# Another order of tasks, and other engines for some of them, in a planned attention and channel-mix kernel

## Chip, core and metric

One core of a Trainium2 chip runs the whole kernel. The metric is the device time in microseconds of one execution; lower is better. The engines are named as in the profile: PE (TensorE), DVE (VectorE), ACT (ScalarE), POOL (GpSimd) and SP (SyncE, which here only issues DMAs).

## What is computed

Block-causal attention over 8 batches, 8 heads, 576 positions and head size 64, and then a channel mix over the attention's output, whose channels are the heads side by side (512).

```python
scores = scale * np.matmul(q, k.transpose(0, 1, 3, 2))
mask = block_i >= block_j                       # blocks of 64 positions
attn = softmax(where(mask, scores, -1e9))
x = (attn @ v).transpose(0, 2, 1, 3).reshape(B, S, H * D)

xk = mu_k * x + (1.0 - mu_k) * x_prev           # x_prev: one position earlier
xr = mu_r * x + (1.0 - mu_r) * x_prev
k = np.maximum(xk @ w_k, 0.0)                   # 512 -> 1024
v = k * k @ w_v                                 # 1024 -> 512
r = 1.0 / (1.0 + np.exp(-(xr @ w_r)))
out = r * v                                     # float32
```

## The kernel before

The kernel is a list of 914 tasks. A task is a few instructions on one engine: a load, a cast, a transpose, a block of matmuls, an exponential. The Python code creates the tasks with what they depend on; two tables then say what is issued. `ORDER` is a list of task numbers: the order in which tasks are issued, and so the order on each engine, which works through its own instructions in that order. A number after a plus sign is a count of fill matmuls (`unread`, L258) on the identity that are put in front of that PE task and whose result nobody reads. `PLACE` has one letter for each task that can run on more than one engine (P for POOL, D for DVE, A for ACT). Buffers come from rings (`RINGS`); a task takes the longest-free slot of a ring at the moment it is issued, so the order decides the slots as well.

The tasks of one batch, by the names used below:

- **Loads** (L266, on SP) of q, k, v and of the weights into one ring of six buffers, `ld`. A buffer is free when its cast is done, and SP issues in order, so a load that waits for a buffer holds all later loads and the stores of the output (L702).
- **Casts** (L245 on ACT, L249 on DVE or POOL, L246 and L250 with a scale) of q and k to bfloat16 (`t_nl`), of v (`t_vo`) and the weights (`WK`, `WR`, `WV`) to float16.
- **Turns** (L332, DVE): 32x32 transposes that bring q and k to head size by position (`t_qkt`).
- **Scores** (L398, PE) into PSUM ring `s` (three buffers), and **exponentials** (L410, ACT) into `t_e`. Batch 0 is done in two parts (positions 0 to 255, and 256 to 575), the others in one, with six units of scores for a batch.
- **Sums** (L460, PE) of the exponentials, a transpose (L486), a reciprocal (L508), small copies (L245 or L249 on `t_rc`) and a second transpose (L533), all on DVE but for some copies; **value groups** A and B (L472, PE); **normalisation** (L543, L547, DVE) into `t_xt`, which gives the PSUM buffers back.
- **Mix**: a difference of neighbouring positions (L570, POOL or DVE), and eight products (L586, DVE) into `XK` and `XR`. They need the mu rows: loaded by L278 (SP, `MUR`), transposed by one small matmul (L285, PE), and shifted by L290 (DVE).
- **Channel mix**: `pk` (L639, PE), **relu** (L612 ACT, L614 DVE), **square** (L621 ACT, L623 DVE or POOL) into `K`; `pr` (L660, PE) and **tanh** (L669, ACT); `pv` (L688, PE), the output product (L696, DVE) and the store. `pk`, `pr` and `pv` share two PSUM buffers, the ring `mm`; relus write a ring `kr` of four.

[...]

Of the kernel before, what the change touches and what calls it, by code (L numbers as in the profile page):

```python
# [19 lines left out]


ORDER = """
# [50 lines left out]
"""  # L73


PLACE = (
    "PDAPPADDAAAPAPDPDPDDPPDAPDAPPDPPDDPPPPPPPPAAPPPAAPPPAAPPPDPPPPDAPDAP"
    "DDAPDAPDPPPAAAAAPPADADPPDDPPAPAPAPAPAPDPDDDPDPAADAAAAPDADPAAAAAAAPAA"
    "DAAAAADPAPAPAPDPAPADAAAAAAADAPAAAPAPAAAADPAPAPAPAPDADPAAAPDPAAAPADAA"
    "AADPAPDPAPAAADAAAADAADDPAPADAPAPADAPAPAPAPADADAPADAD"  # L80
)


# [683 lines left out]
```

## Time and profile before

| | |
|---|---|
| Median of three executions | 262.45 us (260.5 to 262.72) |
| Profiled execution, its own time | 262.48 us |
| Its span, first to last instruction | 260.7 us |
| Mean granted clock of TensorE | 0.991 |
| Moved by DMA | 43.51 MB, read and written |
| Instructions of PE | 3551 matmuls, 3551 weight loads |

A row of a timeline has start, duration, engine, line, operation, output from input, and in square brackets how long the engine had been idle and what it waited for. A row of groups has, after the shapes and the count, busy time and mean ns of one, and then the idle time ahead of it. "issue" as a releaser means that the engine waited for nothing that the profile shows. Line numbers are those of the kernel's file.

### The profile page before, as it was taken

The numbers are of one execution on the slowest core, as the hardware profiler recorded it, in microseconds if no ns is written. First come the engines' busy times: TensorE is split into PE (matmuls) and PEld (weight loads), VectorE is DVE, ScalarE is ACT, GpSimd is POOL, SyncE is SP. The second block draws the span as 40 slices with busy tenths as digits, with TensorE's granted clock in tenths as the row PEclk, the third lists the DMA queues.
The fourth block names the chain that finished last, engine by engine and source line by source line (L and its number), as shares of the span: only waits on it lengthen the run. The fifth ranks groups of instructions, "written<-read, shape, count | busy, mean of one in ns | idle before, by whom it ended". The sixth has DMA issues, their size and how long they took to land.

```text
span 260.7 us, 8212 instructions
## 1 busy us (share of the span) xinstructions
PE 242.8 (93%) x3551; PEld 126.5 (49%) x3551; DVE 200.6 (77%) x286; ACT 175.1 (67%) x257; POOL 110.6 (42%) x96
## 2 busy tenths in 40 slices
PE   1989889898899999999999999999999999989994
PEld 0343565453355436644554665445535654434442
DVE  2658799988999978987799979986788797661322
ACT  1394898566998878898958695988948460554220
POOL 3133563754387532971344447003470452372300
PEclk9997999999999999999999999999999999999998
DMA  7998798999959999949910692030013600400232
GB/s 270 313 350 249 210 303 306 211 271 286 267 191 230 182 358 283 205 168 276 219 41 0 146 308 76 23 140 3 3 43 98 159 0 0 161 4 0 80 140 102
DMA packets 50275, 43.51 MB, mean 167 GB/s; under 512 B 38840, under 2 KB 39104, under 8 KB 50240
## 3 DMA queue, kind: packets, MB, share of 16 engines
q1 hardware_dynamic: 50240, 43.00, 59.7%
q8 instruction: 27, 0.44, 0.8%
q14 instruction: 8, 0.07, 0.1%
HBM read 33.56 MB, written 9.44 MB: 165 GB/s over the span
## 4 chain that ended last, share of the span: by engine, by line
PE 73%; DMA 8%; DVE 8%; POOL 3%; issue 3%; SPq 3%; ACT 2%; DVEq 0%; POOLq 0%
PE t_mm L639 21%; PE t_mm L688 18%; PE t_mm L660 11%; PE t_s L472 7%; PE t_s L398 7%; PE t_mm L258 4%; PE t_s L460 4%; DVE XK L586 3%; DMA out_dram<-t_o 2%; DMA t_ld<-in_moe_w_v_dram 2%; DMA t_ld<-in_moe_w_r_dram 2%; POOL t_d L570 2%; SPq L266 1%; DVE XR L586 1%; DMA MUR<-in_moe_mu_r_dram 1%
## 5 line engine op out<-in xcount | busy, mean ns | idle before, releaser
L410 ACT ACTIVATE t_e<-t_s 128x1024 f16<-128x1024 f32 (+2 forms) x98 | 89.5, 956 | 23.5 <-PE t_s L398 23.2
L623 POOL TENSOR_TENSOR K<-t_kr 128x512 f16<-128x512 f32 (+3 forms) x42 | 43.8, 1054 | 81.0 <-DVE t_kr L614 21.6
L639 PE MATMUL t_mm<-XK,WK 128*128 128x512 f16 (+5 forms) x416 | 70.7, 314 | 1.7 <-ACT t_kr L612 0.7
L688 PE MATMUL t_mm<-WV,K 128*128 128x512 f16 (+1 forms) x296 | 66.7, 373 | 0.6 <-DVE t_o L696 0.6
L612 ACT ACTIVATE t_kr<-t_mm 128x512 f32<-128x512 f32 (+3 forms) x62 | 34.4, 566 | 31.0 <-PE t_mm L639 29.6
L639 PEld LDWEIGHTS <-WK 128*128 128x128 f16 x416 | 36.1, 97 | 31.0 <-issue 7.8
L688 PEld LDWEIGHTS <-K 128*128 128x128 f16 x296 | 28.1, 98 | 33.8 <-issue 3.1
L332 DVE STREAM_TRANSPOSE t_qkt<-t_nl 128x576 f32<-128x576 f32 x32 | 38.8, 1247 | 5.5 <-POOL t_nl L249 3.5
L696 DVE SCALAR_TENSOR_TENSOR t_o<-t_t,t_mm 128x512 f32<-128x512 f32 (+1 forms) x37 | 24.7, 670 | 21.4 <-PE t_mm L688 18.0
L570 POOL TENSOR_TENSOR t_d<-t_xt 128x1152 f32<-128x1152 f32 (+2 forms) x15 | 29.3, 1956 | 20.0 <-DVE t_xt L547 17.1
L398 PE MATMUL t_s<-t_qkt 32*64 32x64 bf16 (+7 forms) x1344 | 33.5, 290 | 2.7 <-DVE t_xt L547 2.1
L660 PE MATMUL t_mm<-WR,XR 128*128 128x512 f16 x144 | 36.0, 380 | 0.0
L669 ACT ACTIVATE t_t<-t_mm 128x512 f32<-128x512 f32 x36 | 21.6, 600 | 15.8 <-PE t_mm L660 15.8
L586 DVE SCALAR_TENSOR_TENSOR XR<-t_d,MU,t_xt 128x576 f16<-128x576 f32 (+2 forms) x36 | 29.5, 837 | 0.1
L398 PEld LDWEIGHTS <-t_qkt 32*64 32x64 bf16 x1344 | 17.7, 105 | 23.5 <-issue 20.7
L586 DVE SCALAR_TENSOR_TENSOR XK<-t_d,MU,t_xt 128x576 f16<-128x576 f32 (+2 forms) x36 | 26.7, 780 | 3.1 <-POOL t_d L570 3.0
L249 POOL CAST t_nl<-t_ld 128x1152 bf16<-128x1152 f32 x17 | 20.4, 1210 | 18.1 <-DVE XR L586 8.2
L533 DVE STREAM_TRANSPOSE t_rt<-t_rc 128x1152 f32<-128x1152 f32 (+2 forms) x18 | 22.3, 1241 | 2.9 <-ACT t_rc L245 2.2
L472 PE MATMUL t_s<-t_e,t_vo 64*64 64x64 f16 (+7 forms) x672 | 22.4, 279 | 1.6 <-issue 1.5
L547 DVE TENSOR_TENSOR t_xt<-t_s,t_rt 128x1024 f32<-128x1024 f32 (+2 forms) x18 | 20.0, 1113 | 1.4 <-PE t_s L472 1.1
L472 PEld LDWEIGHTS <-t_vo 64*64 64x64 f16 x672 | 15.7, 107 | 10.5 <-issue 4.9
L660 PEld LDWEIGHTS <-XR 128*128 128x128 f16 x144 | 12.9, 97 | 15.2 <-issue 1.7
(41 smaller groups left out, 151.7 us busy)
## 6 DMA issues: line engine op xcount, KB each, us to landing
t_ld<-in_k_dram SPq DMA_DIRECT2D x16, 576.0 KB, 5.8
t_ld<-in_q_dram SPq DMA_DIRECT2D x16, 576.0 KB, 6.4
out_dram<-t_o SPq DMA_DIRECT2D x35, 256.0 KB, 2.7
t_ld<-in_v_dram SPq DMA_DIRECT2D x28, 288.0 KB, 5.8
t_ld<-in_moe_w_k_dram SPq DMA_DIRECT2D x4, 512.0 KB, 6.9
t_ld<-in_moe_w_v_dram SPq DMA_DIRECT2D x4, 512.0 KB, 6.4
t_ld<-in_moe_w_r_dram SPq DMA_DIRECT2D x2, 512.0 KB, 5.8
t_ld<-in_v_dram SPq DMA_DIRECT2D x8, 80.0 KB, 5.4
```

The lines of the kernel that those rows point to most:

```text
L332: nc.vector.transpose(new(qkt_buf[b])[:, n, g].rearrange("c s h -> c (s h)").bitcast(FP).rearrange("c (p j) -> c j p", j=JL), new(nl)[:, : ...
L398: nc.tensor.matmul(new(m[r % 2])[g * D:g * D + D, r // 2, col:col + n], qkt[rows, 1, g, t * D:t * D + D, h], qkt[rows, 0, g, q0:q0 + n, h] ...
L410: nc.scalar.activation(new(ebuf[b, part, y, i])[:, :, 0:width], new(m[y])[:, :, 0:width], AF.Exp, scale=ISQ)
L472: nc.tensor.matmul(dst(slice(y * D, (y + 1) * D), u, x, q0, n), new(vo_buf[b])[u * D:u * D + D, 2 * x + y, t], new(ebuf[key])[u * D:u * D ...
L570: return e.tensor_tensor(new(d)[:, 0:2 * n].rearrange("p (u t) -> p u t", u=2), x[:, :, 1 + lo:1 + hi], x[:, :, lo:hi], ALU.subtract)
L586: return nc.vector.scalar_tensor_tensor((XK, XR)[kr][:, cc, g:g + w], new(d)[:, u * n + at - lo:u * n + at - lo + w], MU1[:, kr, cc:cc + 1 ...
L612: nc.scalar.activation(new(kr)[:, 0:w], new(m)[:, 0:w], AF.Relu)
L623: return e.tensor_tensor(dst, KR, KR, ALU.mult)
L639: nc.tensor.matmul(ps[:, a:e], WK[:, cc, jc * P:(jc + 1) * P], XK[:, cc, at:at + e - a], start=(cc == 0), stop=(cc == CCn - 1))
L660: nc.tensor.matmul(ps, XR[:, cc, g % R:g % R + P], WR[:, cc], start=(cc == 0), stop=(cc == CCn - 1))
L688: nc.tensor.matmul(ps[:, 0:w], K2[:, jc, g % RK:g % RK + P], WV[:, jc, cols], start=(jc == 0), stop=(jc == JCn - 1))
L696: nc.vector.scalar_tensor_tensor(new(o)[:, 0:w], new(tb)[:, cols], 1.0, new(m)[:, 0:w], ALU.add, ALU.mult)
```

## The change

Only `ORDER` and `PLACE` are other tables; tasks, buffers, rings and dependencies are the same. [...]

```diff
 ORDER = """
-26 32 0 23 1 27 29 35 28 24 33 3 5 30 34 25 31 2 37 43+20 44 45 46+3 48
+26 0 32 23 27 29 33 24 35 28 34 30 25 31 43+20 45 44 46+3 47 48 106 5 37
...
 PLACE = (
-    "PDAPPADDAAAPAPDPDPDDPPDAPDAPPDPPDDPPPPPPPPAAPPPAAPPPAAPPPDPPPPDAPDAP"
+    "APAPPDAAADPDAPDPPPDDPDDAPDPPPPPPDAPDDPPPPPADPPPPPAPPAADPAPPADADAPDPP"
```

By engine: 11 relus and 7 squares more on ACT; 11 relus fewer and 4 squares more on DVE; 11 squares fewer on POOL, and 4 casts of q and k more; two differences go from POOL to DVE; one weight cast goes from DVE to ACT. There are 53 fill matmuls where there were 54; the 20 in front of the first scores stay.

On PE, at the program's start, the mu rows' transpose (`MUR`) stands first, ahead of the 20 fill matmuls (`identb`). Before:

```order
0 L762 UNCONDITIONAL_BRANCH
1 L285 MATMUL t_mm_153<-identf,MUR 128x8
2 L258 LDWEIGHTS identb
3 L258 MATMUL t_mm_154<-identb 128x512
4 L258 LDWEIGHTS identb
```

And now, where the first sums of batch 0 end (`pick`) and the next fills and scores follow:

```order
323 L460 LDWEIGHTS pick
324 L460 MATMUL t_mm_153<-t_e_85,pick 32x64
325 L285 MATMUL t_mm_154<-identf,MUR 128x8
326 L258 LDWEIGHTS identb
327 L258 MATMUL t_s_148<-identb 128x512
328 L258 LDWEIGHTS identb
329 L258 MATMUL t_s_148<-identb 128x512
330 L398 LDWEIGHTS t_qkt_74
331 L398 MATMUL t_s_148<-t_qkt_74 64x320
```

The transpose moved behind 20 fills, three units of scores and the sums, so the first fills are PE's first work. On SP the two loads of the mu rows moved from third place to second.

On DVE, from the difference of batch 0's second part (`t_d`) to the next batch's turns. Before:

```order
43 L570 TENSOR_TENSOR t_d_122<-t_xt_103 128x640
44 L586 SCALAR_TENSOR_TENSOR XK<-t_d_121,MU_171,t_xt_103 128x320
45 L586 SCALAR_TENSOR_TENSOR XK<-t_d_122,MU_171,t_xt_103 128x320 x2
46 L586 SCALAR_TENSOR_TENSOR XK<-t_d_121,MU_171,t_xt_103 128x320
47 L250 TENSOR_SCALAR WV<-t_ld_63 128x1024
48 L586 SCALAR_TENSOR_TENSOR XR<-t_d_122,MU_171,t_xt_103 128x320
49 L586 SCALAR_TENSOR_TENSOR XR<-t_d_121,MU_171,t_xt_103 128x320
50 L614 TENSOR_SCALAR t_kr_126<-t_mm_154 128x320
51 L614 TENSOR_SCALAR t_kr_127<-t_mm_153 128x320
```

And now:

```order
40 L570 TENSOR_TENSOR t_d_121<-t_xt_103 128x640
41 L586 SCALAR_TENSOR_TENSOR XK<-t_d_122,MU_171,t_xt_103 128x320 x2
42 L586 SCALAR_TENSOR_TENSOR XK<-t_d_121,MU_171,t_xt_103 128x320 x2
43 L249 CAST t_nl_67<-t_ld_61 128x1152
44 L586 SCALAR_TENSOR_TENSOR XR<-t_d_122,MU_171,t_xt_103 128x320 x2
45 L586 SCALAR_TENSOR_TENSOR XR<-t_d_121,MU_171,t_xt_103 128x320 x2
46 L250 TENSOR_SCALAR WV<-t_ld_58 128x1024
47 L332 STREAM_TRANSPOSE t_qkt_74<-t_nl_67 128x18x32
```

The relus (L614) that followed the products are gone from DVE; a cast of batch 2's q stands between the products. The relus are on ACT now, among batch 1's exponentials (`t_e`), tanh (`t_t`) and the casts of `WV`. ACT before:

```order
39 L410 ACTIVATE t_e_92<-t_s_148 128x1024
40 L410 ACTIVATE t_e_93<-t_s_147 128x1024
41 L246 ACTIVATE WV<-t_ld_59 128x1024
42 L246 ACTIVATE WV<-t_ld_61 128x1024
43 L669 ACTIVATE t_t_135<-t_mm_153 128x512
```

And now:

```order
41 L669 ACTIVATE t_t_134<-t_mm_154 128x512
42 L410 ACTIVATE t_e_91<-t_s_147 128x1024
43 L612 ACTIVATE t_kr_127<-t_mm_154 128x320
44 L612 ACTIVATE t_kr_129<-t_mm_153 128x320
45 L246 ACTIVATE WV<-t_ld_62 128x1024
46 L612 ACTIVATE t_kr_128<-t_mm_154 128x320
47 L410 ACTIVATE t_e_93<-t_s_147 128x1024
```

Three relus and a cast of `WV` moved in ahead of the last exponentials of batch 1.

More of the change, by code (lines that the diff above doesn't have):

```diff
@@ L22 @@
 ORDER = """
[50 rows of a table removed]
[50 rows of a table added]
 """
 PLACE = (
-    "PDAPPADDAAAPAPDPDPDDPPDAPDAPPDPPDDPPPPPPPPAAPPPAAPPPAAPPPDPPPPDAPDAP"
-    "DDAPDAPDPPPAAAAAPPADADPPDDPPAPAPAPAPAPDPDDDPDPAADAAAAPDADPAAAAAAAPAA"
-    "DAAAAADPAPAPAPDPAPADAAAAAAADAPAAAPAPAAAADPAPAPAPAPDADPAAAPDPAAAPADAA"
-    "AADPAPDPAPAAADAAAADAADDPAPADAPAPADAPAPAPAPADADAPADAD"
+    "APAPPDAAADPDAPDPPPDDPDDAPDPPPPPPDAPDDPPPPPADPPPPPAPPAADPAPPADADAPDPP"
+    "PAPADDPPPAAPPAADPPDPDPPPDAPPAPAAAAAPDPAPAPAAAPAAAAAAAAAAAAAADAAPAPAA"
+    "APAAAAAAAPDAAAAPAAAAAAAPAPAPADAPAAADAPAPAAAAAPAPAPADAAADAADADPAAAAAD"
+    "AADADDADADAPAPAPAAADADAPAPADAPAPADAPADAAAAAPADAPADAD"
 )
```

98 rows, old and new, of the table ORDER are left out of this document.

## The prediction

> **What bounds the kernel now.** I read the page's engine shares first, then the stretches of the span, then the chain that ended last.
>
> ```profile
> PE 242.8 (93%) x3551; PEld 126.5 (49%) x3551; DVE 200.6 (77%) x286; ACT 175.1 (67%) x257; POOL 110.6 (42%) x96
> ```
>
> ```profile
> 5.95:12.43 6.48, 6.48 (x21) 2.38 (x20) 4.75 (x6) 2.31 (x2) 1.15 (x2) 1.00 1.07 326
> 20.10:49.00 28.90, 25.57 (x548) 15.11 (x548) 26.03 (x44) 23.17 (x32) 15.20 (x17) 0.94 0.82 259
> 49.00:74.00 25.00, 23.08 (x341) 11.42 (x333) 22.49 (x33) 17.69 (x26) 13.33 (x12) 1.00 1.06 244
> 74.00:100.00 26.00, 25.13 (x424) 12.43 (x420) 23.93 (x30) 21.38 (x35) 14.86 (x12) 1.00 1.09 257
> 100.00:211.00 111.00, 110.87 (x1836) 60.90 (x1827) 95.20 (x123) 86.86 (x128) 46.13 (x36) 1.00 0.46 124
> 211.00:260.70 49.70, 45.31 (x224) 20.54 (x212) 23.44 (x33) 16.07 (x28) 15.31 (x11) 0.99 0.17 64
> ```
>
> Each row is a stretch in us, its length, then the busy time of PE, PE's weight loads, DVE, ACT and POOL (instructions in brackets), the granted clock, the DMA share and GB/s. From 100 to 211 us TensorE idles 0.13 us of 111, so there only PE's own work counts, and the change leaves that work as it is (the same matmuls in another order). What can move lies before 100 and behind 211. Between 20.1 and 74 us DVE is busy 26.03 + 22.49 = 48.5 of 53.9 us (90%), while PE idles 3.33 + 1.92 us and in the first part runs fill matmuls besides. There DVE is the tightest engine, and the chain says so too:
>
> ```profile
> 45.66 0.89 DVE t_kr L614 x2
> 46.59 0.38 PE t_mm L258
> ...
> 63.66 0.82 DVE XK L586
> ...
> 64.55 2.63 POOL t_d L570
> ...
> 67.20 1.55 DVE XK L586 x2
> ...
> 69.35 2.19 DVE XR L586 x3
> 71.53 0.55 DVE t_kr L614
> ...
> 72.12 1.67 PE t_mm L639 x8
> ```
>
> Columns: start, us, what. Twice a relu on DVE (L614) stands behind token-mix products (L586) and TensorE waits for it: at 46.59, and at 72.12.
>
> **The start.** Here the change moves the transposed matmul of the mu rows (L285) from ahead of the first 20 fill matmuls to behind the first sums.
>
> ```profile
> 5.78 0.24 PE L285 MATMUL t_mm<-identf,MUR 8*128 8x8 f32 x1 [5.78 <-DMA MUR<-in_moe_mu_r_dram]
> 5.95 6.55 PE L258 MATMUL t_mm<-identb 128*128 128x512 bf16 x20
> 9.77 0.15 PEld L258 LDWEIGHTS <-identb 128*128 128x128 bf16 x1 [0.27 <-issue]
> 10.18 1.83 PEld L258 LDWEIGHTS <-identb 128*128 128x128 bf16 x9 [0.27 <-issue]
> 10.78 1.26 DVE L332 STREAM_TRANSPOSE t_qkt<-t_nl 128x576 f32<-128x576 f32 x1 [0.90 <-ACT t_nl L245]
> 12.43 0.49 PE L398 MATMUL t_s<-t_qkt 32*64 32x256 bf16 x32
> 1.34 0.16 DVE L225 CAST identf<-identb 8x8 f32<-8x8 bf16 x1 [1.34 <-POOL identb masks.py:199]
> ```
>
> Before, the fills ran 5.95 to 12.50. The last turn ended at 12.04, so the fills themselves held the first scores back to 12.43. Without the wait for MUR they can start when identb is there, about 1.4 us (row of 1.34), and last the same 6.55 us: to about 8. The q and k loads are issued in the same order (the 0.6 us of mu issues now stand ahead of the second k load, which moves behind the first anyway), the last cast is still ACT's, so the last turn still ends about 12.05. The gain is 12.43 - 12.05 = **0.4 us**. But PE now idles 8 to 12.05, 4 us, and that is dear:
>
> ```profile
> 20.11 0.28 PE L472 MATMUL t_s<-t_e,t_vo 64*64 64x128 f16 x8 [1.53 <-issue]
> 20.40:23.80 3.40, 3.40 (x39) 1.25 (x40) 3.23 (x6) 0.75 (x2) 1.70 (x2) 0.50 1.11 336
> 24.00:25.00 1.00, 1.00 (x13) 0.34 (x19) 1.00 (x3) 1.00 (x2) 0.36 (x1) 1.00 0.37 66
> ```
>
> An idle of 1.53 us was followed by 3.4 us at half clock, granted 0.50, and full clock behind it. Behind 4 us of idle I expect half clock too, from 12.05 on, for as long as that row shows (3.4 us) or as long as the first fills were slow (5.95 to 10.18, 4.2 us: loads 0.4 us apart up to there, nine in 1.83 behind it). Half of that is lost: 1.7 to 2.1 us, all of it ahead of the first sums, for the scores in between and their fills alternate without a gap. I take **+1.7**; nothing (the array stays warm) is the lower end.
>
> [...]
>
> The 1.53 us itself is "issue": no semaphore held it, in the middle of one task's matmuls.
>
> ```profile
> q8 instruction: 27, 0.44, 0.8%
> ```
>
> 27 instruction transfers of 0.44 MB / 27 = 16 KB each fed the span, and 20.11 is where TensorE ran into one that was late. Counted in PE's instructions, the place stays inside the second value group of batch 0's first part (B before, A now), so I keep the stall: 0, with +1.0 as the upper end (the block before it is worked off sooner than the transfer comes) and -1.5 as the lower.
>
> [...]
>
> **The stretch from 20 to 74 us.** What moves between the engines up to the sums of batch 2, by the mean of each form:
>
> ```profile
> L249 DVE CAST t_nl<-t_ld 128x1152 bf16<-128x1152 f32 x6 | 5.1, 845 | 0.0
> L250 DVE TENSOR_SCALAR WV<-t_ld 128x1024 f16<-128x1024 f32 x2 | 1.4, 685 | 0.0
> L614 DVE TENSOR_SCALAR t_kr<-t_mm 128x256 f32<-128x256 f32 x3 | 1.3, 422 | 1.3 <-PE t_mm L639 1.1 <-POOL K L623 0.2
> L614 DVE TENSOR_SCALAR t_kr<-t_mm 128x320 f32<-128x320 f32 x4 | 1.9, 484 | 0.2 <-PE t_mm L639 0.2
> L614 DVE TENSOR_SCALAR t_kr<-t_mm 128x448 f32<-128x448 f32 x2 | 1.1, 616 | 0.0
> L570 DVE TENSOR_TENSOR t_d<-t_xt 128x1152 f32<-128x1152 f32 x2 | 2.8, 1388 | 0.0
> L570 DVE TENSOR_TENSOR t_d<-t_xt 128x640 f32<-128x640 f32 x1 | 0.8, 819 | 0.0
> L249 DVE CAST t_vo<-t_ld 128x640 f16<-128x640 f32 x1 | 0.5, 479 | 0.0
> ```
>
> DVE loses there nine relus (3 x 0.42 + 4 x 0.48 + 2 x 0.62 = 4.4), one square and one v cast (0.9 together, by the 256-wide relu's row and the v cast's own): 5.3. It gains two differences of the token mix (1.39 for batch 1, and 0.7 for a 512-wide one, between nothing and the 640-wide one's 0.82) and two relus (0.42 + 0.62): 3.1. Of casts of 0.85 and 0.69 as many come as go, but for one that stands in DVE's idle start; a pair of small copies that goes isn't counted. Net 5.3 - 3.1 = **-2.2 us** of DVE. What hides what: ACT gets the relus and about five squares between the exponentials, and idles 5.7 + 7.3 = 13 us in these two stretches, so it has room, but in a fixed order. The difference of batch 1 stood in the chain for POOL's 2.63 us while DVE did other work; now DVE does it itself in 1.39, and the products behind it wait no longer for POOL. The two waits for relus, and the one for scores:
>
> ```profile
> PE t_mm L258 <- DVE t_kr L614: 1.3, 1, 1.3
> PE t_mm L639 <- DVE t_kr L614: 0.2, 1, 0.2
> PE t_s L398 <- DVE t_xt L547: 2.1, 2, 1.1
> ```
>
> The last row, scores that wait for a normalisation to give PSUM back (2.1 us in two waits), I expect to stay: PE issues the scores of batch 2 after the second group of batch 1 as before. I take DVE's **-2.2** and count the 1.5 us of relu waits as a part of it, since they are what DVE's work made late; what is late next is ACT, whose relus now stand behind exponentials of about 1 us. The ends are 0 (ACT is as late as DVE was) and -3.7 (both sums).
>
> **74 to 211 us.** PE idles 0.87 + 0.13 us there, so no more than 1.0 is to be gained.
>
> ```profile
> L612 ACT ACTIVATE t_kr<-t_mm 128x512 f32<-128x512 f32 x47 | 27.7, 598 | 26.7 <-PE t_mm L639 25.5 <-POOL K L623 1.2
> ```
>
> ACT gets about five relus more there, 5 x 0.6 = 3 us, and is busy 21.38 + 86.86 = 108 of 137 us: covered. DVE and POOL lose a little. I take 0, with -0.8 and +1.8 as ends (a new PE wait of one ACT relu, 0.6 us, three times; if the cover were gone altogether it would be the 3 us).
>
> **Behind 211 us.** From the last value groups of batch 7 on (211 us), PE's order is the same, instruction for instruction. One wait can go:
>
> ```profile
> 228.94 1.97 POOL K L623
> 230.93 0.61 ACT t_kr L612
> ```
>
> A square on POOL that took 1.97 us while DVE squared held a relu, and TensorE paused behind it. POOL had nine squares in this tail, now seven, ACT takes two. I take **-0.4**, between 0 and -0.9; the others are placed as they were.
>
> **The sum.** Against this execution's own 262.48 us (span 260.7 and 1.78 around it; the runs' median is 262.45): -0.4 + 1.7 + 0 - 2.2 + 0 - 0.4 = -1.3, **261.2 us**.
>
> **Rivals.** First, *DVE's relief is worth its whole size* and the clock costs nothing, as the fills at half clock only use time in which PE would wait for exponentials: -0.4 - 2.2 - 1.5 - 0.4 = -4.5, 258.0. For it speaks DVE's 90% over 54 us; against it PE's own 25.57 us of work in 28.9, fills among it. Second, and on the other side, *the half clock carries through*: the first sums are 2.1 us late, the late instruction block comes 1.0 later still, and ACT, which now has relus and weight casts between the exponentials of batch 1, can't give it back, so DVE starts its dense stretch 3.1 - 0.4 us later and ends it the same: 262.5 + 2.7 + 0.3 for one more ACT wait = 265.5. It decides from the point where DVE's dense stretch starts more than 2.6 us later than now, since DVE's 2.2 and the tail's 0.4 can pay that much. For it speaks that DVE has only 5.4 us idle up to 74; against it that the weight loads come earlier, as POOL, not ACT behind its exponentials, now frees the buffers of batch 1's q and k. Third, *it cancels*: the plan only renames what PE waits for, and the gain at 46 us is what the start lost: 262.5. For it speaks that 111 of 261 us are PE alone.
>
> **How the numbers follow.** A measurement of this kernel tells about 1% (2.6 us) from no change. My forecast, with its own range of -0.3 to -3.5, 0.40; cancelling (within 1 us about 262.5, or a little above) 0.20; relief of its whole size 0.22; half clock carried through 0.18. Three tenths of the forecast lie under 259.8 (the relu waits beside DVE's relief, or the tail whole), so faster by over 1% has 0.22 + 0.12 = 0.34; slower by over 1% (above 265.1) takes 0.14 of the second rival and 0.02 of cancelling; the rest, 0.50, is within. The range reaches from the whole relief with the idle 1.0 us of 74 to 211 as well, 257.0, to the slow rival's 265.5.
>
> **What would show it.** Fills from 1.4 to 8 us, then a gap, and granted clock 0.5 at the first scores (right: sums of batch 0 one to two us later than now). DVE's share between 20 and 74 us lower by 2 to 3 us, no PE wait for L614 at 45 to 48 us. PE without idle from 100 to 211. The forecast is wrong if the clock is full at 12 us, if PE waits for ACT's relus or exponentials between 30 and 60 us by more than 2 us, or if a new wait of over 1.5 us stands behind 100 us.

## The result, and the profile after

The changed kernel takes 260.77 us (median, 259.07 to 265.02), the kernel before 262.64 us on the same chip (260.5 to 264.58): a ratio of 0.9935, 95% interval 0.9906 to 0.9964. (The medians are of all runs; the ratios, here and below, leave out runs in the slow state, of which the changed kernel had four.) That is 1.9 us less where 1.3 were forecast. The profiled execution is one of the quickest, 259.07 us, so the two profiles differ by 3.4 us; where a size matters below, the runs' ratio decides, and the traces tell the place.

The page's engine shares and the stretches, with the same bounds and columns as those shown of before:

```profile
PE 242.2 (94%) x3550; PEld 126.9 (49%) x3550; DVE 194.4 (76%) x280; ACT 179.1 (70%) x272; POOL 96.1 (37%) x87
```

```profile
12.43:20.10 7.67, 6.25 (x144) 3.18 (x143) 1.93 (x4) 3.60 (x7) 2.81 (x3) 0.55 1.04 307
20.10:49.00 28.90, 25.53 (x535) 14.79 (x535) 25.69 (x46) 26.04 (x42) 13.96 (x16) 1.00 0.89 295
49.00:74.00 25.00, 24.11 (x466) 13.18 (x465) 23.01 (x31) 22.10 (x37) 11.05 (x11) 1.00 1.08 250
74.00:100.00 26.00, 25.88 (x426) 13.11 (x424) 22.20 (x27) 23.31 (x34) 14.58 (x12) 1.00 0.97 270
100.00:211.00 111.00, 110.84 (x1763) 60.54 (x1763) 95.25 (x129) 85.65 (x129) 40.15 (x31) 1.00 0.46 118
```

Between 20.1 and 74 us DVE is busy 48.7 us, as before (48.5): the relief does not show as less work in these bounds, but as work that comes earlier. TensorE idles 0.89 us in 49 to 74 where it idled 1.92, and 0.12 in 74 to 100 where it idled 0.87. The start is worse: the granted clock is 0.55 on average in 12.43 to 20.10. TensorE's waits and its first rows (timeline: start, duration, operation, idle before):

```profile
PE t_s L398 <- DVE t_qkt L332: 5.6, 2, 3.5
PE t_mm L660 <- ACT WV L246: 1.6, 1, 1.6
PE t_mm L258 <- POOL identb masks.py:199: 1.4, 1, 1.4
PE t_mm L258 <- ACT t_kr L612: 0.7, 1, 0.7
```

```profile
1.36 6.58 PE L258 MATMUL t_mm<-identb 128*128 128x512 bf16 x20 [1.36 <-POOL identb masks.py:199]
11.48 0.27 PE L398 MATMUL t_s<-t_qkt 32*64 32x256 bf16 x1 [3.54 <-DVE t_qkt L332]
13.85 0.76 PE L398 MATMUL t_s<-t_qkt 32*64 32x256 bf16 x31 [2.09 <-DVE t_qkt L332]
14.54 1.46 PE L258 MATMUL t_mm<-identb 128*128 128x512 bf16 x3
...
16.62 1.46 PE L258 MATMUL t_mm<-identb 128*128 128x512 bf16 x3
18.01 1.08 PE L398 MATMUL t_s<-t_qkt 32*64 32x320 bf16 x48
19.01 0.57 PE L460 MATMUL t_mm<-t_e,pick 128*32 128x128 f16 x24
```

```profile
12.53 1.26 DVE L332 STREAM_TRANSPOSE t_qkt<-t_nl 128x576 f32<-128x576 f32 x1 [1.10 <-ACT t_nl L245]
```

The fills run from 1.36 as forecast, and the scores stand at half clock (granted 0.50 in 13.80 to 18.00, three fills in 1.46 us). But the last turn starts at 12.53, not 10.78: the first full scores come 1.4 us later, not 0.4 earlier, and the sums at 19.01, 3.2 us later. Yet the sums of batch 0's second part stand at 33.73 against 33.69. Behind them, at the seventh `pk` of batch 0's second part (columns of 320), both are still about level (54.93 and 54.58). So the gain lies behind 54 us, and begins with batch 1's normalisation (L543). DVE's rows there, of the kernel before and then of the changed one:

```profile
55.34 0.49 DVE L614 TENSOR_SCALAR t_kr<-t_mm 128x320 f32<-128x320 f32 x1 [0.17 <-PE t_mm L639]
55.86 0.76 DVE L249 COPY t_rc<-t_rc 32x36 f32<-32x36 f32 x4
56.65 1.38 DVE L533 STREAM_TRANSPOSE t_rt<-t_rc 128x1152 f32<-128x1152 f32 x1
59.45 0.29 DVE L543 TENSOR_TENSOR t_xt<-t_s,t_rt 128x128 f32<-128x128 f32 x1 [1.43 <-PE t_s L472]
```

```profile
55.03 0.36 DVE L249 COPY t_rc<-t_rc 32x36 f32<-32x36 f32 x2
55.43 1.38 DVE L533 STREAM_TRANSPOSE t_rt<-t_rc 128x1152 f32<-128x1152 f32 x1
56.91 0.29 DVE L543 TENSOR_TENSOR t_xt<-t_s,t_rt 128x128 f32<-128x128 f32 x1
```

The normalisation comes 2.54 us earlier, in two parts of about equal size: the transpose ahead of it 1.22 (a relu and two copies fewer, 0.9 of it), and an idle time of 1.43 of which 0.10 is left. That wait is a matter of the order alone. TensorE's rows, again of before and of after, show the two value groups (L472):

```profile
55.77 1.42 PE L472 MATMUL t_s<-t_e,t_vo 64*64 64x64 f16 x40
...
59.18 1.42 PE L472 MATMUL t_s<-t_e,t_vo 64*64 64x64 f16 x40
```

```profile
55.57 1.42 PE L472 MATMUL t_s<-t_e,t_vo 64*64 64x64 f16 x40
...
58.11 1.42 PE L472 MATMUL t_s<-t_e,t_vo 64*64 64x64 f16 x40
```

Group A's result was there at 57.2 before, too. But group B's first matmuls write their first columns into the PSUM buffer of the sums, which A's normalisation reads. The old table issues task 143 (group B) ahead of task 148 (A's normalisation), so that read waits for B's first matmuls: 59.18 and 0.27 behind it, 59.45. The new table issues 148 nine places ahead of 143, and nothing is waited for but A. The runs of the next section agree, all of them: in the six profiles whose table issues 143 first, this normalisation starts 0.27 or 0.28 us behind B's first matmul; in the eight that issue 148 first, it starts 1.20 to 1.35 us ahead of it.

In the tables below "seam" is the start of that seventh `pk` of batch 0's second part and "tail" that of `pv` 27, some 45 us from the end. Ahead of each of these two points TensorE has done exactly the same tasks in all kernels (fill matmuls aside), so the times can be compared. Times in us, from the trace of one execution each:

| kernel | sums, batch 0 | norm. A, batch 0 | sums, 2nd part | seam | norm. A, batch 1 | sums, batch 2 | tail | last pv |
|---|---|---|---|---|---|---|---|---|
| before | 15.81 | 20.51 | 33.69 | 54.58 | 59.46 | 73.73 | 215.50 | 256.18 |
| after | 19.02 | 22.58 | 33.73 | 54.93 | 56.91 | 72.34 | 213.13 | 252.73 |

From the seam to the tail the changed kernel gains 2.7 us (158.20 for 160.92), from the tail to the last `pv` 1.1 (39.60 for 40.68).

### The profile page after: what moved, and what is told of

Its sections match the earlier page's. It is cut to its first block, busy times and chain, and to the rows that moved or that the text cites. A ratio compares the mean times of both kernels' runs of the same rounds, so it can differ in the third digit from the quotient of the medians.

```text
span 257.0 us, 8209 instructions
## 1 busy us (share of the span) xinstructions
PE 242.2 (94%) x3550; PEld 126.9 (49%) x3550; DVE 194.4 (76%) x280; ACT 179.1 (70%) x272; POOL 96.1 (37%) x87
## 4 chain that ended last, share of the span: by engine, by line
PE 72%; DMA 8%; ACT 8%; DVE 7%; issue 2%; SPq 1%; POOL 0%; DVEq 0%; POOLq 0%
PE t_mm L688 23%; PE t_mm L639 20%; PE t_mm L660 11%; PE t_s L398 8%; PE t_s L472 6%; DMA t_ld<-in_v_dram 5%; ACT t_e L410 4%; DMA t_ld<-in_q_dram 3%; PE t_s L460 2%; ACT t_kr L612 1%; PE t_mm L258 1%; DVE t_xt L547 1%; DVE XK L586 1%; DVE t_qkt L332 1%; ACT t_nl L245 1%
## 5 line engine op out<-in xcount | busy, mean ns | idle before, releaser
L639 PE MATMUL t_mm<-XK,WK 128*128 128x512 f16 (+5 forms) x416 | 69.7, 314 | 0.9 <-ACT t_kr L612 0.4
L612 ACT ACTIVATE t_kr<-t_mm 128x512 f32<-128x512 f32 (+3 forms) x73 | 39.6, 554 | 24.9 <-PE t_mm L639 22.8
L623 POOL TENSOR_TENSOR K<-t_kr 128x512 f16<-128x512 f32 (+3 forms) x31 | 30.4, 989 | 45.9 <-DVE XR L586 20.0
L249 POOL CAST t_nl<-t_ld 128x1152 bf16<-128x1152 f32 x21 | 23.8, 1147 | 53.3 <-DVE XK L586 13.4
L570 POOL TENSOR_TENSOR t_d<-t_xt 128x1152 f32<-128x1152 f32 (+2 forms) x13 | 25.5, 1961 | 8.3 <-DVE t_xt L547 7.4
L586 DVE SCALAR_TENSOR_TENSOR XR<-t_d,MU,t_xt 128x576 f16<-128x576 f32 (+2 forms) x36 | 26.9, 767 | 0.1
L249 POOL CAST t_vo<-t_ld 128x1152 f16<-128x1152 f32 (+2 forms) x13 | 13.4, 1040 | 26.8 <-DVE XR L586 12.3
L472 PE MATMUL t_s<-t_e,t_vo 64*64 64x64 f16 (+7 forms) x672 | 22.4, 279 | 0.0
L547 DVE TENSOR_TENSOR t_xt<-t_s,t_rt 128x1024 f32<-128x1024 f32 (+2 forms) x18 | 20.1, 1114 | 2.8 <-PE t_s L472 1.3
```

The costliest lines, as they stand in the source:

```text
L249: return e.tensor_copy(dst, src)
L472: nc.tensor.matmul(dst(slice(y * D, (y + 1) * D), u, x, q0, n), new(vo_buf[b])[u * D:u * D + D, 2 * x + y, t], new(ebuf[key])[u * D:u * D ...
L570: return e.tensor_tensor(new(d)[:, 0:2 * n].rearrange("p (u t) -> p u t", u=2), x[:, :, 1 + lo:1 + hi], x[:, :, lo:hi], ALU.subtract)
L586: return nc.vector.scalar_tensor_tensor((XK, XR)[kr][:, cc, g:g + w], new(d)[:, u * n + at - lo:u * n + at - lo + w], MU1[:, kr, cc:cc + 1 ...
L612: nc.scalar.activation(new(kr)[:, 0:w], new(m)[:, 0:w], AF.Relu)
L623: return e.tensor_tensor(dst, KR, KR, ALU.mult)
```

## The experiments

Three theories were set against each other. *Absorbed*: what the start loses or gains is taken up by the late instruction block before it reaches batch 1. *Relief*: DVE's removed relus are the gain, as my sum had it. *One plan*: order and engines fit only each other, and the gain lies in a few places of the order.

### The start: warmer, or with the old load order

The changed kernel with 46 fills for 20, so that TensorE idles less ahead of the scores:

```diff
-26 0 32 23 27 29 33 24 35 28 34 30 25 31 43+20 45 44 46+3 47 48 106 5 37
+26 0 32 23 27 29 33 24 35 28 34 30 25 31 43+46 45 44 46+3 47 48 106 5 37
```

> The changed kernel with 46 fill matmuls instead of 20 ahead of the first scores, so that TensorE stays busy until they can start (20 fills ended at 7.94 us, the scores ran from 13.85 on; 26 x 0.2135 us = 5.6 us). Both theories: granted clock full at the first scores, the first sums about 1.5 us earlier than 19.0 us. Theory 'absorbed' (the lateness of the start is gone by the second part's sums at 33.7 us, which stand at the same time before and after): total as the changed kernel, 260.8 within 0.5 us. Theory 'carried' (each us of the start is a us of the end): 259.3.

Measured 263.1 us, ratio to the kernel before 1.0009 (0.9976 to 1.0041): slower than the changed kernel by some 0.7%, which neither theory had. TensorE still idles 2.00 us, between the first matmul of the scores and the others (13.04 to 15.05), but the scores run at full clock (granted 1.00 in 12.43 to 20.10, three fills in 0.82 us). The changed kernel with the mu loads in third place, as before:

```diff
-26 0 32 23 27 29 33 24 35 28 34 30 25 31 43+20 45 44 46+3 47 48 106 5 37
+26 32 0 23 27 29 33 24 35 28 34 30 25 31 43+20 45 44 46+3 47 48 106 5 37
```

> The changed kernel with the two mu loads back in third place on SP, behind the second k load, and nothing else. Both theories: the last turn of batch 0's first part ends near 12.0 us instead of 13.8, the first scores run at half clock from 12.1 on, the sums are 1.7 us earlier than 19.0. Absorbed: 260.8 within 0.5 us. Carried: 259.1.

Measured 260.07 us, 0.9894 (0.9856 to 0.9932). Both edits together, with 38 fills:

```diff
-26 0 32 23 27 29 33 24 35 28 34 30 25 31 43+20 45 44 46+3 47 48 106 5 37
+26 32 0 23 27 29 33 24 35 28 34 30 25 31 43+38 45 44 46+3 47 48 106 5 37
```

> Both at once: mu loads third, and 38 fills. First sums near 15.9 us as in the kernel before. Absorbed: 260.8 within 0.5 us. Carried: 257.6. If the start is only partly absorbed, in between, and the time at which the second part's sums start (33.7 us) moves by as much as the end does.

Measured 260.56 us, 0.9918 (0.9883 to 0.9953). And the other side, the kernel before with the mu rows' transpose and the shift behind it (tasks 1 and 2) moved behind the first sums, so that its fills come at 1.36 and the clock falls:

```diff
-26 32 0 23 1 27 29 35 28 24 33 3 5 30 34 25 31 2 37 43+20 44 45 46+3 48
-4 38 109 36 110 73+3 47 74 75 49 6 70+3 71 50 51+1 52 72 53 79+4 80 81 7
+26 32 0 23 27 29 35 28 24 33 3 5 30 34 25 31 37 43+20 44 45 46+3 48
+4 38 109 36 110 73+3 47 74 75 49 1 2 6 70+3 71 50 51+1 52 72 53 79+4 80 81 7
```

> The kernel before, with the mu rows' transpose and its shift moved behind batch 0's first sums, mu loads left third: the change's clock step alone. Fills from 1.4 to 8 us, scores at 12.1 us at half clock, first sums 1.5 to 2 us later than 15.8. Absorbed: as the kernel before, 262.6 within 0.5 us. Carried, and as the prediction's term had it: +1.3, 263.9.

Measured 262.49 us, 1.0005 (0.9973 to 1.0037). Its window, with the clock as third number from the end, and the next one:

```profile
12.43:20.10 7.67, 6.97 (x169) 3.66 (x176) 1.98 (x4) 4.50 (x6) 2.81 (x3) 0.62 1.09 310
20.10:23.80 3.70, 3.58 (x97) 1.81 (x82) 3.39 (x10) 2.49 (x4) 0.47 (x1) 1.00 0.94 344
```

The half clock is there, the sums come at 18.04 for 15.81, and the end does not move. Two things take the delay up, and the first is the late instruction block: the last weight load ahead of it starts at 20.95 for 18.23, the first one of it at 21.43 for 20.11, so 1.4 of 2.7 us are gone. The second is the half clock that the kernel before has behind its idle time there (0.50 in 20.40 to 23.80); this kernel idles 0.12 us in 20.10 to 23.80 and has 1.00, and its scores at 24.71 are ahead of the other's at 24.95. By the sums of the second part it is 0.6 us behind again (34.27 for 33.69), for reasons that I did not follow.

That is one pair of traces. Every run lists its mean granted clock, and by it the average hides two cases. Of the runs that the ratios count, the kernel before took 262.0 us on average in 30 at 0.997 to 1.000, and 263.5 in 31 at 0.991 to 0.993, which is one stretch of 3.4 us at half clock more (1.7 of 260 us); the kernel with the late transpose took 262.1 in six at 0.991 to 0.993 and 263.4 in six at 0.984 to 0.987. So the end stays where it is on average because the kernel before often pays for a half-clock stretch too; against its runs without one, a start with two such stretches is some 1.4 us late.

TensorE's first rows behind the late block, of 46 fills, of 38 with the old load order, and of 20 with the old load order:

```profile
23.53 0.39 PE L258 MATMUL t_s<-identb 128*128 128x512 bf16 x1 [3.26 <-ACT WK L245]
```

```profile
21.49 0.95 PE L472 MATMUL t_s<-t_e,t_vo 64*64 64x192 f16 x25 [2.54 <-issue]
```

```profile
22.78 0.28 PE L472 MATMUL t_s<-t_e,t_vo 64*64 64x128 f16 x7 [1.17 <-issue]
```

Each is weight load 223 of the program (counted from 0), the first of its block: the late loads of all profiles are numbers 223, 479, 607 and 863, multiples of 128 apart (in the first 63 us). It is named after whatever else came last, ACT in the first; but in all of them the 16 KB transfer of the block had landed 1.30 to 1.55 us earlier (22.09, 19.95, 21.48; before: 18.78 for 20.11). With the old load order and 38 fills the sums come at 16.16, 2.3 us ahead of those with 20 fills, and TensorE then stands 2.54 us: the normalisation is 0.63 earlier and the end not at all.

The changed kernel with the old load order and no fills ahead of the first scores (`43+20` to `43`):

> The changed kernel with the mu loads third and none of the 20 fills ahead of the first scores: 40 instructions fewer on PE, so the third instruction block's first instruction moves 20 matmuls further on in the work, behind both value groups of batch 0's first part. Theory 'late block' (the block comes at 20 to 23.5 us whatever PE does before, and PE stands there: 0.3 to 3.6 us of wait in five kernels, each time at weight load 223): the value groups no longer wait, their normalisation starts 1 to 1.5 us earlier than 23.17 us in the kernel with 20 fills, the wait stands later and is shorter; 259.3 if that carries on, against 260.1 with the fills. Rival (the fills warm the array for what follows): the scores are slower than with 20 fills, first sums later than 18.5 us, 260.5 or more.

Measured 263.48 us, 1.0015 (0.9977 to 1.0053), so about 3 us worse than with 20 fills. Its rows:

```profile
12.28 0.76 PE L398 MATMUL t_s<-t_qkt 32*64 32x256 bf16 x31 [1.53 <-DVE t_qkt L332]
12.97 1.46 PE L258 MATMUL t_mm<-identb 128*128 128x512 bf16 x3
14.36 0.76 PE L398 MATMUL t_s<-t_qkt 32*64 32x192 bf16 x32
15.05 0.98 PE L258 MATMUL t_mm<-identb 128*128 128x512 bf16 x3
...
22.47 0.41 PE L398 MATMUL t_s<-t_qkt 32*64 32x320 bf16 x23 [1.29 <-issue]
...
37.76 0.44 PE L472 MATMUL t_s<-t_e,t_vo 64*64 64x192 f16 x15 [2.96 <-issue]
```

It is not the warmth that the fills bought: the normalisation of batch 0 comes at 19.93, 3.2 us earlier than with them, and the sums of the second part are 2.0 us ahead. What turns it round is another block. Its first load (479) stands in value group A of batch 0's second part, 20 loads later in it than with the fills, and there TensorE's loads are 3.23 us apart (the last row), the transfer having landed 1.34 us before the second of them. With the fills that transfer had landed at 32.60, 3.3 us ahead of need; here it landed at 36.42. So without the 20 fills the boundary falls 20 loads later in the work, and there it turns a lead of 2.0 us into a lag of 1.8 at the seam (57.28 for 55.52); why its transfer came later was not shown.

| kernel | sums, batch 0 | norm. A, batch 0 | sums, 2nd part | seam | last pv |
|---|---|---|---|---|---|
| 46 fills | 18.41 | 24.71 | 36.98 | 58.74 | 257.26 |
| mu third | 18.46 | 23.17 | 34.31 | 55.52 | 253.22 |
| mu third, 38 fills | 16.16 | 22.54 | 34.45 | 56.04 | 255.63 |
| mu third, no fills | 16.66 | 19.93 | 32.28 | 57.28 | 256.95 |
| before, transpose late | 18.04 | 22.56 | 34.27 | 55.15 | 257.33 |

### Order without engines, engines without order, and the relus alone

The old order with the new engines (the whole `PLACE` of the changed kernel):

```diff
 PLACE = (
-    "PDAPPADDAAAPAPDPDPDDPPDAPDAPPDPPDDPPPPPPPPAAPPPAAPPPAAPPPDPPPPDAPDAP"
+    "APAPPDAAADPDAPDPPPDDPDDAPDPPPPPPDAPDDPPPPPADPPPPPAPPAADPAPPADADAPDPP"
...
```

> The order of before with the engines of the change. Theory 'relief' (what the change gains between 49 and 100 us and behind 211 us, 3.5 us of the two profiles' difference, comes from work taken off DVE): most of it stays, PE's wait for the relu L614 at 46 us is gone, 260.5 to 261.5. Theory 'order' (it comes from what PE is given to do while it would wait): 262.6 or above, since ACT's added relus stand where the old order puts them.

And the new order with the old engines:

> The order of the change with the engines of before. Relief: no gain, 262.6 or above, with the relus back on DVE behind the products. Order: 260.5 to 261.5.

Measured 289.23 us, 1.1006 (1.0946 to 1.1065), and 285.18 us, 1.0869 (1.0813 to 1.0926). Both are far off what any part of either theory gives: neither table has a gain that the other doesn't need. A smaller cut, the kernel before with the nine relus up to batch 2's sums (74 us) on ACT:

```diff
-    "DDAPDAPDPPPAAAAAPPADADPPDDPPAPAPAPAPAPDPDDDPDPAADAAAAPDADPAAAAAAAPAA"
-    "DAAAAADPAPAPAPDPAPADAAAAAAADAPAAAPAPAAAADPAPAPAPAPDADPAAAPDPAAAPADAA"
+    "DDAPDAPDPPPAAAAAPPADADPPDDPPAPAPAPAPAPAPADAPAPAAAAAAAPAAAPAAAAAAAPAA"
+    "AAAAAAAPAPAPAPDPAPADAAAAAAADAPAAAPAPAAAADPAPAPAPAPDADPAAAPDPAAAPADAA"
```

> The kernel before with only the nine relus up to batch 2's sums moved from DVE to ACT: the prediction's largest term by itself. Relief: PE's 1.3 us wait for L614 at 46.6 us goes, batch 2's sums start 1 to 2 us earlier than 73.7, total 260.4 to 261.6. Rival (ACT is late instead, the relus standing behind exponentials of 1 us): sums at 73.7 or later, 262.6 or more.

Measured 269.01 us, 1.0253 (1.0192 to 1.0313). TensorE's waits:

```profile
PE t_mm L258 <- ACT t_kr L612: 4.3, 2, 3.7
PE t_mm L639 <- ACT t_kr L612: 3.1, 2, 2.3
```

DVE lost the 4.4 us that my sum counted, and the kernel is 2.5% or 6.6 us slower, for ACT does the relus behind exponentials that its old order puts first, and behind its idle time TensorE runs at a granted 0.50 in 34.4 to 37.8 and in 51.5 to 54.8 besides. The relief alone is no gain. Its mirror, the changed kernel with the same nine relus back on DVE:

```diff
-    "PAPADDPPPAAPPAADPPDPDPPPDAPPAPAAAAAPDPAPAPAAAPAAAAAAAAAAAAAADAAPAPAA"
-    "APAAAAAAAPDAAAAPAAAAAAAPAPAPADAPAAADAPAPAAAAAPAPAPADAAADAADADPAAAAAD"
+    "PAPADDPPPAAPPAADPPDPDPPPDAPPAPAAAAAPDPDPDPDADPAADAAAAADADAAADAAPAPAA"
+    "DPAAAADAAPDAAAAPAAAAAAAPAPAPADAPAAADAPAPAAAAAPAPAPADAAADAADADPAAAAAD"
```

> The changed kernel with its nine early relus (three of batch 0, four of batch 1, two of batch 2) back on DVE, in its own order. DVE gets 4.4 us of work, ScalarE loses as much. By my prediction's term (DVE's time between 20 and 74 us is what counts) the kernel ends 3 to 4.4 us later: 264 to 265, ratio to the kernel before 1.005 to 1.01. By the theory that order and engines are one plan, each relu now stands on DVE behind products that its order never meant to be ahead of it, and TensorE waits for relus as it did in the mirror image (nine relus on ScalarE in the old order, 6 us): 266 to 269, ratio 1.013 to 1.025. If DVE has room there after all, the time stays at 260.8.

Measured 266.61 us, 1.014 (1.009 to 1.019); against the changed kernel's 0.9935 that is about 5 us, more than the 3 to 4.4 of DVE's added time, and at the lower end of what "one plan" expected. The seam is at 57.75, the tail at 219.09. So in the new order DVE's relief is needed, in the old one it is dear. The way that "one plan" named isn't what the trace shows, though: TensorE waits only 1.7 us for these relus (0.7, 0.6 and 0.4). A stretch at 0.50 (34.45 to 37.8), a wait of 1.7 for a tanh and one of 1.0 for a block stand beside it, and how the 5 us divide was not separated.

### The order by stretches

With the seam and the tail the tables can be spliced. The old tables up to the seam, the new ones behind it (the lines at the splice):

```diff
...
-733 517 169 739 161 162 118 163 734 524 525 189 191 141 119 533 527 120
-142 526 528 219 144 529 222 534 121 190 532 173 518 741 145 519 536 520
+733 517 169 739 161 162 118 163 734 524 525 189 191 141 533 144 119 142
+120 534 146 225 526 190 532 145 147 148 222 216 121 149 151 535 518 536
...
```

> Both tables have a place, 196 or 197 tasks in, up to which they issue the same tasks but one (about 54 us on TensorE, where both profiles stand within 0.2 us of each other). This kernel takes order and engines of the kernel before up to there, and those of the changed kernel behind it. By the theory of stretches (what is gained lies behind the seam, and can be had without the new start) it ends 2 to 3 us earlier than the kernel before: ratio 0.988 to 0.993, and batch 2's sums come about 1.4 us earlier than before, the last output products about 3 us. By its rival, that a table works only as a whole (both mixed kernels lost 9 or 10%), new waits of TensorE appear behind the seam and the ratio is over 1.01.

The new tables up to the seam, the old ones behind it (against the changed kernel):

```diff
...
-132 140 168 517 172 166 169 189 191 734 524 739 141 525 118 533 144 119
+132 140 168 517 172 166 169 189 191 734 524 739 141 525 118 523 119 533
...
```

> The other half: order and engines of the changed kernel for its first 196 tasks, those of the kernel before behind them. By the theory of stretches the new start is worth nothing by itself: its half clock and later mu loads are paid for by the late instruction block and by waits that follow anyway, so the ratio is 1.000, within 0.004, although the engines' work of 20 to 54 us is already the new one (nine relus on ScalarE). If DVE's relief of the first 54 us were the source of the gain, it would be 0.988 to 0.993. By the rival that a table works only as a whole it is over 1.01.

The old tables up to the tail, the new ones for the last 111 tasks:

```diff
-840 481 852 479 480 854 820 486 866 489 867 484 868 869 487 863 482 858
+840 481 852 479 480 854 820 486 866 868 487 489 867 869 482 484 863 864
...
-    "AADPAPDPAPAAADAAAADAADDPAPADAPAPADAPAPAPAPADADAPADAD"
+    "AADPAPDPAPAAADAAAADAADAPAPADAPAPADAPADAAAAAPADAPADAD"
```

> Order and engines of the kernel before for its first 803 tasks (up to about 210 us; here both tables have issued exactly the same tasks), those of the changed kernel for the last 111. By the two profiles the tail is worth 1.1 us: ratio 0.996 and TensorE's pause at 229 us gone. My prediction had 0.4 us there: 0.9985. By the rival that the tail is hidden behind the output products and the last store, 1.000.

| kernel | us | ratio to before | seam | norm. A, batch 1 | sums, batch 2 | tail | last pv |
|---|---|---|---|---|---|---|---|
| new behind the seam | 260.06 | 0.9893 (0.9852 to 0.9935) | 54.70 | 57.19 | 72.73 | 214.92 | 254.45 |
| new up to the seam | 265.06 | 1.009 (1.0056 to 1.0125) | 56.80 | 62.56 | 76.83 | 218.43 | 259.09 |
| new for the tail | 261.41 | 0.9934 (0.9899 to 0.9969) | 55.16 | 60.03 | 74.31 | 216.07 | 255.89 |

The new order behind the seam gives the whole gain, or more, without the new start; the new start without the rest costs 2.4 us (1.5 to 3.3). Of the first of the three, DVE's rows right behind the splice:

```profile
55.71 1.38 DVE L533 STREAM_TRANSPOSE t_rt<-t_rc 128x1152 f32<-128x1152 f32 x1
57.19 0.29 DVE L543 TENSOR_TENSOR t_xt<-t_s,t_rt 128x128 f32<-128x128 f32 x1
```

Here six of the nine early relus are on DVE as before, and the seam is at the old time (54.70); still the normalisation is 2.3 us earlier than in the kernel before, with no wait. The wait stays where the old order runs behind the new start. DVE's wait row of "new up to the seam":

```profile
DVE t_xt L543 <- PE t_s L472: 1.3, 1, 1.3
```

No run moved that one task alone, so its share is read from the traces: 1.3 to 1.4 of the 2.3 to 2.5 us. Of these the sums of batch 2 keep 1.0 to 1.4, for TensorE had other work in between. In the spliced kernel one wait eats part of it at 77 us, for a v cast on POOL:

```profile
PE t_s L472 <- POOL t_vo L249: 1.5, 1, 1.5
```

From the seam to the tail the spliced kernel's trace is then 0.7 us shorter than before (160.23 for 160.92), where the changed kernel's is 2.7.

The tail is the cleanest cut. TensorE's rows, of before and of the spliced tail:

```profile
226.79 4.05 PE L639 MATMUL t_mm<-XK,WK 128*128 128x512 f16 x18
231.58 2.79 PE L639 MATMUL t_mm<-XK,WK 128*128 128x512 f16 x12 [0.74 <-ACT t_kr L612]
```

```profile
226.63 7.45 PE L639 MATMUL t_mm<-XK,WK 128*128 128x512 f16 x33
```

The pause is gone, and from the tail to the last `pv` the trace is 0.86 us shorter (39.82 for 40.68). By the runs the tail is worth 1.7 us, but the interval (0.8 to 2.7) takes in 0.86.

The spliced kernel (260.06) and the changed kernel with the old load order (260.07) are the quickest run here. Their intervals overlap that of the changed kernel, so a gain over it isn't shown; the two ideas were not run together.

## Why the prediction was right, and where it was right by luck

**The total** held: 1.9 us for 1.3. Its two large terms stand for other things than I said, and part of the agreement is luck: start and clock, +1.3 us in my sum, were +3.2 at the first sums and 0.0 at those of the second part, and the gain that follows is not the one that I counted. Of the signs that I named, the early fills, the half clock, and the vanished wait for L614 at 46 us came; DVE's time between 20 and 74 us, which was to fall by 2 to 3 us, did not (48.7 for 48.5).

**The start's -0.4** failed at its step on SP: "the 0.6 us of mu issues now stand ahead of the second k load, which moves behind the first anyway". It does not. The second k load is issued 0.7 us later (1.89 for 1.19), and its turn starts at 8.74 for 6.96; with the loads back in their place it starts at 7.01 and the sums come 0.56 us earlier. That pair is too small a measure: the last cast of q, which the scores wait for, starts at 9.41 to 10.79 us in the nine profiles with the mu loads third, and at 10.82 to 12.55 in the five with them second, 1.5 us later on average. Why 0.7 us of issue becomes 1.5 of landing was not shown.

**The clock's +1.7** was right in its size on the spot: from the first full scores to the sums, 5.16 us for 3.37, so 1.8. But "lost" was wrong. The kernel before with the same half clock ends where it ended on average (1.0005), because the late block stood next in line, and behind it a half-clock stretch of the kernel before's own. The step that failed is to add a delay to the end without asking what waits behind it; I had put the late block in a term of its own, at 0, instead of letting the two overlap. So the second rival, half clock carried through with 3 us, falls as a mechanism; only against runs of the kernel before without any half clock does some 1.4 us of it show at the end. That the new start alone still costs 2.4 us has other parts: the mu loads, and what of the new order around the first value groups I could not separate. The same 196 tasks reached the seam at 54.93 in one profile and at 56.80 in another, 0.5 us of it from a later cast (first full scores at 13.85 and 14.35) and the rest from the block (weight load 223 at 22.19 and at 24.08). By scatter of this size the profile of the changed kernel looks better than its median.

**The late block's 0** (from -1.5 to +1.0): 0.3 us of it is left in the profile of the changed kernel, 1.0 to 1.7 in the four other kernels that start in the new order with 20 fills. A second one, which I hadn't looked for, costs 1.58 at 41.95. It is shown as a wait for ACT's `WV`, but it is weight load 607, the first of its block, and the transfer had landed at 40.64. In the kernel with the old load order this block is in time, and TensorE waits 1.7 us for a tanh a moment later: it wasn't on top of the rest. Of the first four boundaries here (weight loads 223 to 607) one or two held TensorE up in thirteen kernels, by 0.3 to 3.6 us, and in the fourteenth none did.

**DVE's -2.2** had a size that the records neither confirm nor exclude (from the seam to the tail 2.7 in the changed kernel's trace and 0.7 in the spliced one's; in the runs 1.1, the difference of 2.8 and 1.7 us, each uncertain by a us) and the wrong cause. Counting instructions moved off the busiest engine gave a number that the nine relus alone turn into +6.6 us. What the traces show to come earlier is batch 1's normalisation, half of it by shorter work ahead of it and half by a dependency that the order no longer makes; how much of that reaches the end, beside the tail's 1.7, the runs do not resolve. I had the row that would have told: the scores' waits for L547, 2.1 us, of which I wrote that I expect them to stay, as the scores come behind group B as before. They do, and both waits went all the same: the one at 63.80, since the normalisation in front of it moved; the one at 39.11 (scores of batch 1), since TensorE now has scores, a `pr` and a value group to do before them (35.30 to 39.70) where it had both value groups in one piece.

**74 to 211** was inside its bounds: TensorE's idle fell by 0.75 in 74 to 100 and there was nearly nothing more to gain.

**The tail's -0.4** was right in its mechanism and too small: the pause of 0.74 us at 231 us is gone as a whole (0.86 by the trace up to the last `pv`), where I took half. Nothing else came late in its place.

Of the rivals, *relief of its whole size* names a cause that costs 6.6 us when it stands alone, though the profiled execution came within 1.1 us of its 258.0; that *it cancels* is spoken against by the interval, which ends 0.9 us below no change.

## What to carry to other kernels

In a kernel whose order is a table, look first at which task is issued ahead of which on a buffer they share: here a read that was issued behind another task's write to the same tile waited for it, though the columns differ, and the row showed DVE idle for 1.43 us (up to 59.45) although group A's result had been there since 57.2. Don't price work moved off the busiest engine by its duration: follow it into the queue of the engine that gets it, for the same nine relus cost 6.6 us in one order and saved 5 in the other. And look at what stands behind a delay: ahead of the late instruction block 1.4 us of 2.7 cost nothing here, while 20 fills fewer put the first load of a later block (479) 20 loads further on in the work, where TensorE's loads then stood 3.23 us apart.

## What was not expected of the hardware

TensorE at half speed need not show in the granted clock of the views. In the kernel without fills the windows of its first scores read 1.00, with three fills in 1.46 us as at a granted 0.50. The trace has no clock record ahead of 15.40 us, and a window counts time without a record as 1.00; the first record stands where the matmuls become fast:

```profile
12.43:14.00 1.57, 1.57 (x34) 0.75 (x25) 0.05 (x1) 0.88 (x2) 1.15 (x1) 1.00 1.25 264
```

Its sums came 4.4 us after the first full scores (16.66 behind 12.28), between the 3.4 at full clock (the kernel before) and the 5.2 of the five kernels that had filled and then idled 2.6 to 3.7 us: filling early and idling was worse than not filling, on this stretch. The kernel before shows slow matmuls without a record as well: its windows read 1.00 up to 20.40, its first record is at 10.16, and its 20 fills start 0.43 us apart up to 10.18 and 0.22 behind it.

Nor did the length of the idle time alone decide on half clock here, as my reading of the one row of 1.53 us had it. It stood behind 1.53 us (the kernel before) and 1.79 (new for the tail) at weight load 223; behind 1.58 there (new behind the seam), 2.32 (nine relus on ACT) and the 2.00 with 46 fills the granted clock stayed at 1.00. The 18 half-clock stretches of the fourteen profiles, those at the very end left out, lasted 3.4 or 6.8 us, every one. What decides is not shown here.

And the late block has its own clockwork: in thirteen kernels TensorE went on with weight load 223 1.27 to 1.62 us after the block's transfer had landed, and that transfer began 1.9 to 4.7 us after TensorE had entered the block before. That block of short matmuls is worked off in 3.1 to 4.5 us, and the next one is late; the following block lasts 8.1 to 10.6 us, and the one behind it (load 351) was in time in all fourteen. In the old order with the new engines the transfer began 0.3 us behind that point, landed at 17.72, and nothing waited.
